# Float64 weights decoded with a parametric ReLU on ScalarE

## Chip, cores and metric

One Trainium2 chip, one of its cores. The metric is the device time of one execution of the program in microseconds; lower is better. PE is TensorE (matmuls; PEld its weight loads), DVE VectorE, ACT ScalarE, POOL GpSimd and SP the engine that issues the DMAs here. L92 is line 92 of the kernel file.

## What is computed

Three layers in a row, in float32 for the activations and with float64 weights:

```python
# attention inside chunks of 64 rows: q, k, v of 8 x 8 x 576 x 64
scores = q_c @ k_c.T / 8;  attn = softmax(scores);  x = attn @ v_c        # -> 8 x 576 x 512
# gated layer with a causal depthwise convolution of 5 taps
gate = sigmoid(sum(conv_w[k] * shift(x, k)));  x = (gate * (x @ w_val)) @ w_out   # 512 x 512 each
# feed-forward with layer norm, 512 -> 2048 -> 512
xn = (x - mean) / sqrt(var + 1e-6) * g_ln;  out = x + relu(xn @ w_ch1) @ w_ch2
```

w_val, conv_w, w_out, g_ln, w_ch1 and w_ch2 may come as float64. The chip gets the 64 bits of such a number as two 32-bit words, a low and a high one.

## The kernel before

**Precision.** Every operand of a large matmul is split in a high part, rounded to the type fp32r, and a low part, the rest. A product takes three matmuls: high by high, high by low, low by high.

**Decoding a weight.** A raw tile of 128 x 512 pairs of words comes by DMA (tag `raw`, two buffers in each pool). Four steps make a float32 tile `a` (tag `da`, three buffers) of it: ACT reads the high word as a float32, whose eight exponent bits are the upper eight of the float64's eleven, and multiplies it by 2^-112 (L87). That clears the top three exponent bits, so that DVE can shift the word left by three (L91). The shift throws the sign out. DVE takes the sign bit out of the high word and ORs it in (L92), then shifts the low word right by 29 and ORs that in (L93). `parts` then makes the two matmul operands: ACT rounds `a` to the high part (L100), POOL subtracts for the low part (L101). For the first feed-forward matrix, SP stores `a` to DRAM (L147) for later use.

**Where decodes run.** 41 times: once small (20 x 128) for the convolution's taps, four times for w_val and four times for w_out in the first 60 us, and 32 times for the feed-forward, two tiles `raw1` and `raw2` for each of 16 slices f of the hidden dimension. The first four slices are decoded when the last block's convolution is done (`early_ff`, issued after `last_tap`), the others by `next_ff` while the first block of rows runs through the feed-forward.

**Stages on PE.** Up to about 290 us: attention, convolution and gated layer, block by block (9 blocks of 512 rows), software-pipelined in `period`. From 290 to 313 us the last projection (`proj`) and the transposes of the first normalised rows. From 313 us the first block's feed-forward: per slice f, `ff1` (12 matmuls into `psh`, then hh on ACT L454 and hl on DVE L455) and `ff2` of an earlier slice (12 matmuls into `acc`), with the layer norm and the transposes of the next rows between them (`ln_rows`, `turn_rows`: the ACT scalings L425 and L435). From 417 us the other eight blocks, two at a time, in eight pairs of slices (`ff_pair`), where a Winograd-like scheme takes 7 products for 8: `make_pair` builds its weight combinations from the stored `a` on DVE (L521 to L524), ACT and POOL (L477, L478); `right_operands` builds those of the rows (L546, L478); inside a pair, `copy` (ACT L626), `add` (DVE L630) and `relu` (ACT L621, DVE L622) stand between the products.

**Order.** PE's order is written out by hand throughout, DVE's and ACT's too in the periods. Elsewhere a planner orders each engine's instructions ahead of time by its own costs and by priorities. Each engine, and SP's DMA queue, runs its instructions in order, so one that waits holds all those behind it.

Of the kernel before, what the change touches and what calls it, by code (L numbers as in the profile page):

```python
# [8 lines left out]
F32 = mybir.dt.float32  # L9
F32R = mybir.dt.float32r  # L10
U32 = mybir.dt.uint32
ACTF = mybir.ActivationFunctionType
ALU = mybir.AluOpType
# [6 lines left out]
def tile_chunk_attention_gated_mlp(ctx: ExitStack, tc: tile.TileContext, qk, v, w_val, conv_w, w_out, g_ln, w1, w2, out):  # L20
    nc = tc.nc
# [22 lines left out]
    scale = 1.0 / float(D) ** 0.5  # L44
# [39 lines left out]
        nc.sync.dma_start(out=t.rearrange("p c h d -> p (c h d)"), in_=v[u])  # L84

    def decode_copy(raw, a):
        nc.scalar.activation(out=a, in_=raw[:, :, 1].bitcast(F32), func=ACTF.Copy, scale=2.0 ** -112)  # L87

    def decode_bits(raw, a):
        lw, hw, au = raw[:, :, 0], raw[:, :, 1], a.bitcast(U32)  # L90
        nc.vector.tensor_scalar(out=au, in0=au, scalar1=3, scalar2=None, op0=ALU.logical_shift_left)  # L91
        nc.vector.scalar_tensor_tensor(out=au, in0=hw, scalar=0x80000000, in1=au, op0=ALU.bitwise_and, op1=ALU.bitwise_or)  # L92
        nc.vector.scalar_tensor_tensor(out=au, in0=lw, scalar=29, in1=au, op0=ALU.logical_shift_right, op1=ALU.bitwise_or)  # L93

    def decode(raw, a):
        decode_copy(raw, a)
        decode_bits(raw, a)
# [611 lines left out]
    def ff_copy(k):  # L709
        a = fa[k] = stg.tile([P, DM], F32, tag="da", name="da", bufs=3)  # L710
        decode_copy(wraw[k // 2][k % 2], a)

    def ff_bits(k):
        decode_bits(wraw[k // 2][k % 2], fa[k])
# [306 lines left out]
```

## Time and profile before

| | before |
|---|---|
| three runs, median (lowest to highest) | 1103.33 us (1102.24 to 1105.18) |
| profiled execution, time | 1105.21 us |
| its span, first to last instruction | 1103.4 us |
| mean granted PE clock | 0.989 |
| PE busy | 1058.8 us (96%), 6778 matmuls |
| DVE busy | 698.6 us (63%), 1107 instructions |
| ACT busy | 499.6 us (45%), 872 instructions |
| POOL busy | 106.2 us (10%), 120 instructions |

The profile is of one execution. Busy times are sums over the whole span; a granted clock of 1.00 is 2.4 GHz and 0.50 is 1.2 GHz.

### The profile page before, as it was taken

The numbers are of one execution on the slowest core, as the hardware profiler recorded it, in microseconds if no ns is written. First come the engines' busy times: TensorE is split into PE (matmuls) and PEld (weight loads), VectorE is DVE, ScalarE is ACT, GpSimd is POOL, SyncE is SP. The second block draws the span as 40 slices with busy tenths as digits, with TensorE's granted clock in tenths as the row PEclk, the third lists the DMA queues.
The fourth block names the chain that finished last, engine by engine and source line by source line (L and its number), as shares of the span: only waits on it lengthen the run. The fifth ranks groups of instructions, "written<-read, shape, count | busy, mean of one in ns | idle before, by whom it ended". The sixth has DMA issues, their size and how long they took to land.

```text
span 1103.4 us, 16877 instructions
## 1 busy us (share of the span) xinstructions
PE 1058.8 (96%) x6778; PEld 862.9 (78%) x6778; DVE 698.6 (63%) x1107; ACT 499.6 (45%) x872; POOL 106.2 (10%) x120
## 2 busy tenths in 40 slices
PE   4899999999899898999999999999999999999998
PEld 3578888888677676888888888888888888888887
DVE  5899999997969987556638335448334447433434
ACT  5777777776756654344433233433233323222221
POOL 1210000000124444222200000000000000000000
PEclk9999999999999898999999999999999999999999
DMA  9534344412387745333335523323533224522211
GB/s 374 204 140 144 136 144 154 144 59 78 115 280 234 240 162 219 134 116 134 135 136 167 173 96 115 117 93 125 200 103 108 97 85 132 194 94 96 77 39 76
DMA packets 58725, 156.32 MB, mean 142 GB/s; under 512 B 5758, under 2 KB 13974, under 8 KB 56214
## 3 DMA queue, kind: packets, MB, share of 16 engines
q1 hardware_dynamic: 58646, 155.23, 40.7%
q8 instruction: 53, 0.87, 0.3%
q14 instruction: 26, 0.21, 0.1%
HBM read 117.46 MB, written 37.75 MB: 141 GB/s over the span
## 4 chain that ended last, share of the span: by engine, by line
PE 79%; DVE 12%; ACT 3%; DMA 3%; issue 2%; POOL 1%; SPq 0%; ACTq 0%; DVEq 0%; POOLq 0%
PE x L610 16%; PE acc L584 16%; PE psf L584 15%; PE zy L610 9%; PE pso L335 8%; PE psv L335 8%; PE sc L175 2%; PE x L250 2%; DVE da L92 2%; DVE h L622 2%; PE pst L218 1%; DMA qkr<-in_qk 1%; DVE da L93 1%; PE pst L433 1%; DVE xt L546 1%
## 5 line engine op out<-in xcount | busy, mean ns | idle before, releaser
L630 DVE TENSOR_TENSOR c<-x,c 128x512 f32<-128x512 f32 x96 | 66.2, 690 | 235.5 <-ACT c L626 179.6
L584 PE MATMUL acc<-w,h 128*128 128x512 f32 x768 | 184.5, 390 | 0.0
L584 PE MATMUL psf<-w,h 128*128 128x512 f32 x768 | 184.3, 389 | 0.0
L584 PEld LDWEIGHTS acc<-w,h 128*128 128x128 f32 x768 | 144.3, 188 | 30.1
L584 PEld LDWEIGHTS psf<-w,h 128*128 128x128 f32 x768 | 144.3, 188 | 29.8
L610 PE MATMUL x<-t,wc 128*128 128x512 f32 x576 | 149.0, 395 | 4.6 <-DVE c L630 4.6
L626 ACT ACTIVATE c<-zy 128x512 f32<-128x512 f32 x96 | 57.8, 602 | 185.2 <-PE zy L610 185.1
L610 PEld LDWEIGHTS x<-t,wc 128*128 128x128 f32 x576 | 109.3, 190 | 28.8 <-DVE c L630 6.2
L621 ACT ACTIVATE h<-c 128x512 fp32r<-128x512 f32 x96 | 60.6, 631 | 134.8 <-DVE c L630 134.2
L589 DVE TENSOR_TENSOR yt<-psf,yt 128x512 f32<-128x512 f32 x128 | 88.1, 690 | 23.5 <-PE psf L584 20.7
L304 DVE SCALAR_TENSOR_TENSOR cg<-xf,cw,cg 128x516 f32<-128x516 f32 (+1 forms) x136 | 100.4, 752 | 3.0
L610 PE MATMUL zy<-b,wc 128*128 128x512 f32 x384 | 99.1, 394 | 0.0
L610 PEld LDWEIGHTS zy<-b,wc 128*128 128x128 f32 x384 | 71.7, 189 | 14.4
L622 DVE SCALAR_TENSOR_TENSOR h<-c,h 128x512 fp32r<-128x512 f32 x96 | 68.0, 708 | 11.2 <-ACT h L621 10.9
L335 PE MATMUL pso<-oh,gh 128*128 128x512 f32 x144 | 58.3, 405 | 1.8 <-ACT gh L371 1.8
L335 PE MATMUL psv<-xh,vh 128*128 128x512 f32 x144 | 59.2, 411 | 0.0
L335 PE MATMUL pso<-oh,gl 128*128 128x512 f32 x144 | 56.9, 395 | 1.9 <-DVE gl L374 1.9
L101 POOL TENSOR_TENSOR w<-da,w 128x512 fp32r<-128x512 f32 x32 | 46.1, 1447 | 114.7 <-ACT w L100 108.7
L335 PE MATMUL pso<-ol,gh 128*128 128x512 f32 x144 | 56.6, 393 | 0.0
L335 PE MATMUL psv<-xl,vh 128*128 128x512 f32 x144 | 56.6, 393 | 0.0
L335 PE MATMUL psv<-xh,vl 128*128 128x512 f32 x144 | 56.6, 393 | 0.0
L621 ACT ACTIVATE h<-x 128x512 fp32r<-128x512 f32 x32 | 19.2, 598 | 81.3 <-PE x L610 81.3
(114 smaller groups left out, 1591.9 us busy)
## 6 DMA issues: line engine op xcount, KB each, us to landing
wc<-wc SPq DMA_DIRECT2D x112, 512.0 KB, 3.2
qkr<-in_qk SPq DMA_DIRECT2D x19, 1024.0 KB, 7.4
raw<-in_moe_w_ch SPq DMA_DIRECT2D x32, 512.0 KB, 4.4
vr<-in_v SPq DMA_DIRECT2D x18, 512.0 KB, 4.2
yd<-y SPq DMA_DIRECT2D x36, 256.0 KB, 2.0
out<-yt SPq DMA_DIRECT2D x36, 256.0 KB, 3.7
yr<-yd SPq DMA_DIRECT2D x32, 256.0 KB, 3.2
yt<-yd SPq DMA_DIRECT2D x32, 256.0 KB, 3.7
```

Source lines behind the costliest of these rows:

```text
L92: nc.vector.scalar_tensor_tensor(out=au, in0=hw, scalar=0x80000000, in1=au, op0=ALU.bitwise_and, op1=ALU.bitwise_or)
L101: nc.gpsimd.tensor_tensor(out=lo, in0=a, in1=hi, op=ALU.subtract)
L175: nc.tensor.matmul(out=ps[CH * c:CH * c + CH, par, g, :], lhsT=qt[r0:r0 + CH, hp, cs], rhs=kt[r0:r0 + CH, hp, cs], start=True, stop=True,)
L304: last_tap[j] = nc.vector.scalar_tensor_tensor(out=o, in0=xf[j][:, f, i:i + n], scalar=cw[:, i * CT + f:i * CT + f + 1], in1=o, op0=ALU.mu ...
L335: nc.tensor.matmul(out=ps, lhsT=lt, rhs=rh, start=(i == 0), stop=(i == n - 1))
L584: nc.tensor.matmul(out=ps, lhsT=lt, rhs=rh, start=(g == 0 and k == 0 and (first or half)), stop=(g == 1 and k == 2 and (last or half)),)
L589: nc.vector.tensor_tensor(out=yt[i], in0=ps, in1=yt[i], op=ALU.add)
L610: nc.tensor.matmul(out=ps, lhsT=lt, rhs=rh, start=(start and c == 0 and i == 0), stop=(c == 1 and i == 2), skip_group_check=True)
L621: nc.scalar.activation(out=t[:, 0, :], in_=src, func=ACTF.Relu)
L622: nc.vector.scalar_tensor_tensor(out=t[:, 1, :], in0=src, scalar=0.0, in1=t[:, 0, :], op0=ALU.max, op1=ALU.subtract)
L626: nc.scalar.activation(out=t, in_=zy, func=ACTF.Copy)
L630: nc.vector.tensor_tensor(out=t, in0=x, in1=t, op=ALU.add)
```

## The change

The multiplication by 2^-112 on ACT becomes a parametric ReLU with the same scale and a slope of 2^32 for negative inputs. A negative number then comes out with 32 added to its exponent, which sets the exponent bit that the left shift by three moves into the place of the sign. So the shift gives the sign as well, and DVE's L92 is left out: a decode has three instructions on ACT and DVE before `parts` where it had four.

```diff
     def decode_copy(raw, a):
-        nc.scalar.activation(out=a, in_=raw[:, :, 1].bitcast(F32), func=ACTF.Copy, scale=2.0 ** -112)
+        nc.scalar.activation(out=a, in_=raw[:, :, 1].bitcast(F32), func=ACTF.Prelu, scale=2.0 ** -112, alpha=2.0 ** 32)
 
     def decode_bits(raw, a):
-        lw, hw, au = raw[:, :, 0], raw[:, :, 1], a.bitcast(U32)
+        lw, au = raw[:, :, 0], a.bitcast(U32)
         nc.vector.tensor_scalar(out=au, in0=au, scalar1=3, scalar2=None, op0=ALU.logical_shift_left)
-        nc.vector.scalar_tensor_tensor(out=au, in0=hw, scalar=0x80000000, in1=au, op0=ALU.bitwise_and, op1=ALU.bitwise_or)
         nc.vector.scalar_tensor_tensor(out=au, in0=lw, scalar=29, in1=au, op0=ALU.logical_shift_right, op1=ALU.bitwise_or)
```

## Rows read from the trace of the kernel before

**Rows 1.** The page's slices: busy tenths of PE and DVE in 40 slices.

```profile
...
PE   4899999999899898999999999999999999999998
...
DVE  5899999997969987556638335448334447433434
...
```

**Rows 2.** Stages: length; PE, PEld, DVE, ACT, POOL busy; clock; DMA; GB/s.

```profile
...
313.00:329.50 16.50, 16.50 (x73) 13.36 (x72) 11.51 (x24) 9.17 (x15) 5.31 (x4) 1.00 0.89 286
329.50:338.20 8.70, 5.32 (x20) 4.07 (x20) 7.90 (x18) 4.56 (x9) 2.59 (x2) 0.80 0.82 261
338.20:370.00 31.80, 31.80 (x151) 26.38 (x149) 31.63 (x61) 21.15 (x47) 14.64 (x10) 1.00 0.76 242
370.00:384.50 14.50, 9.45 (x33) 7.41 (x33) 13.19 (x17) 10.32 (x23) 7.53 (x5) 0.76 0.71 231
384.50:402.70 18.20, 16.96 (x75) 13.36 (x73) 15.90 (x25) 8.93 (x21) 7.47 (x6) 1.00 0.61 203
...
417.30:440.00 22.70, 17.61 (x62) 12.83 (x61) 15.87 (x25) 9.08 (x20) 9.74 (x12) 0.85 0.70 266
...
```

**Rows 3.** Groups by line, 313 to 403 us: busy, mean ns, idle before.

```profile
...
L101 POOL TENSOR_TENSOR w<-da,w 128x512 fp32r<-128x512 f32 x27 | 38.6, 1437 | 54.6 <-ACT w L100 48.6 <-issue 6.0
...
L92 DVE SCALAR_TENSOR_TENSOR da<-raw,da 128x512 uint32<-128x512 uint32 x26 | 24.7, 953 | 0.3
...
L87 ACT ACTIVATE da<-raw 128x512 f32<-128x512 f32 x26 | 17.2, 668 | 3.9 <-DMA raw<-in_moe_w_ch 3.9
...
```

**Rows 4.** Busy time by stage, instructions of L92 alone.

```profile
...
338.20:370.00 31.80, 10.02 (x11) 1.00 0.76 242
370.00:384.50 14.50, 6.60 (x6) 0.76 0.71 231
...
```

**Rows 5.** PE's waits, 284 to 440 us: total us, times, longest.

```profile
...
PE x L610 <- DVE c L630: 4.6, 3, 2.6
PE pst L433 <- ACT xt L435: 3.4, 1, 3.4
PE psh L335 <- ACT w L100: 2.8, 1, 2.8
PE pso L335 <- DVE gl L374: 1.9, 1, 1.9
...
PE psh L335 <- DVE hl L455: 1.7, 1, 1.7
...
```

**Rows 6.** Groups by line of the whole program, ACT.

```profile
...
L425 ACT ACTIVATE yr<-yr,w,r 128x512 f32<-128x512 f32 x32 | 24.4, 808 | 20.0 <-DVE w L423 19.9
...
L621 ACT ACTIVATE h<-x 128x512 fp32r<-128x512 f32 x32 | 19.2, 598 | 81.3 <-PE x L610 81.3
...
L198 ACT ACT_TABLE_LOAD x7 | 9.0, 1283 | 0.1
...
```

**Rows 7.** The line L92: ns shortest, median, longest.

```profile
...
L92 DVE SCALAR_TENSOR_TENSOR da<-raw,da x40: 650/692/1770, 11.4 to 399.9; 128x512 uint32<-128x512 uint32 x40
...
```

**Rows 8.** Timeline of DVE, 9 to 25 us: start, length.

```profile
...
10.47 0.28 DVE L92 SCALAR_TENSOR_TENSOR cwr<-cwu,cwr 20x128 uint32<-20x128 uint32 x1
...
11.44 0.69 DVE L92 SCALAR_TENSOR_TENSOR da<-raw,da 128x512 uint32<-128x512 uint32 x1
...
```

**Rows 9.** Chain that ended last, 9 to 24 us: start, length.

```profile
...
12.47 10.62 DMA qkr<-in_qk
...
23.13 1.23 PE x L284 x2
```

**Rows 10.** Chain that ended last, 57 to 63 us.

```profile
...
58.57 1.28 ACT L198
...
```

**Rows 11.** Timeline of DVE, 306 to 330 us.

```profile
...
324.92 0.69 DVE L92 SCALAR_TENSOR_TENSOR da<-raw,da 128x512 uint32<-128x512 uint32 x1
...
```

**Rows 12.** Timeline of ACT, 375 to 390 us.

```profile
...
376.21 0.63 ACT L100 ACTIVATE w<-da 128x512 fp32r<-128x512 f32 x1 [0.91 <-DVE da L93]
...
378.29 0.36 ACT L435 ACTIVATE xt<-pst,cw 128x128 f32<-128x128 f32 x1
...
```

## Prediction

> **What bounds the kernel.** I read the page's slices first. PE is busy in 39 of the 40 slices at eight tenths or more, and DVE is full in slices 3 to 9 and again in slices 13 to 15, from 331 to 414 us [rows 1]. A change that only relieves DVE can therefore gain nothing except where PE waits, so the next view is the busy time by stage around those slices, where the last weights (the feed-forward's) are decoded while the first block runs [rows 2]. The stretch from 313 to 329.5 us sets the pace: 73 matmuls in 16.5 us at clock 1.00 and without a gap, 0.226 us each. At that pace the 20 matmuls of the next stretch need 4.5 of its 8.7 us, so 4.2 us are lost there. The 33 of 370 to 384.5 need 7.5 of 14.5: 7.0 lost. The 75 of 384.5 to 402.7 need 17.0 of 18.2: 1.2 lost. These are the least that is lost, as some of the matmuls are short transposes. Between them, from 338.2 to 370, PE is never idle, but DVE has only 0.17 of 31.80 us free. From 417.3 to 440 another 8.7 us go (62 matmuls). Part of each loss is the clock: 0.80, 0.76 and 0.85 in the three bad stretches. The granted clock falls from 2.4 towards 1.2 GHz after PE has been kept waiting, so a wait that goes takes its slow matmuls with it.
>
> What the decode costs there is in the groups by line [rows 3]: from 313 to 403 us the merge of the sign, L92, takes 24.7 us of DVE in 26 instructions. The stretches of L92 alone say how much stands in the full queue: 11 before 370 and 6 up to 384.5 [rows 4]. The view of PE's waits names who ends them [rows 5]: the scaling of the transposed rows xt L435 (3.4 us), the high half of a weight w L100 (2.8), hl L455 (1.7), gl L374 (1.9), and c L630 (4.6 in three).
>
> **The change, part by part.** Removed: 41 L92 instructions (40 of 128x512, and the small one of the convolution's weights). Nothing is added to DVE. On ACT, 41 Copy become 41 Prelu at the same place. The trace has no Prelu. Below it stands Relu into h, 598 ns, above it the 128x512 ACTIVATE with two per-partition operands, 808 ns [rows 6]; the Copy it replaces takes 668 [rows 3]. I take 668, since scale and slope are both plain numbers; the dearer end would add 0.14 us to each of 26 in a stage where ACT is busy 54 of 90 us (the sum over 313 to 402.7 in [rows 2]), so it hides. No DMA, tile or buffer moves, but both successors do: L93 can start one instruction earlier, and with it w L100, POOL's w L101, the store of a and, as L93 is the last reader of raw, the next weight load on SP's queue.
>
> How long is one removed L92? Its mean in the stage is 953 ns, yet its shortest is 650 and its median over the program 692, its longest 1770 [rows 3, 7]; the long ones run beside POOL's L101, of 1437 ns each. If that wait belongs to L92, 24.7 us go; if L93, which stands behind it and also reads two SBUF tensors, inherits it, only 26 x 0.69 = 18.0 go. I count 0.69, which goes in either case; with the whole record term 5 below would reach its upper bound, 7.0, and the sum 13.0 in place of 11.5. Both figures are above the 12.4 us (4.2 + 7.0 + 1.2) that PE loses in the stage, so the cap on the gain is what PE loses and not the DVE time that comes free. The Trainium skill, SBUF — State Buffer, section "SBUF: two separate sides", says that VectorE and GpSimd hold a shared port pair for a whole instruction, so the loser waits it out. By that rule the wait passes on to L93, which speaks for 18.0 and the sum of 11.5, and makes the change worth less than the row's mean says; the spread from 650 to 1770 ns agrees with such waits, and who inherits them only the changed kernel can show.
>
> The terms, in order of time:
> (1) Start. DVE runs an L92 of 0.28 and one of 0.69 us [rows 8] ahead of the first normalisation, for which PE's first transposes wait. PE then runs into the next load of q and k, which lands at 12.47 + 10.62 = 23.09 [rows 9]; PE starts the matmuls just ahead of those that need it at 23.13 and takes 1.2 us for them, so about 1 us of earlier work still counts. 1.0; bounds 0 and 1.0.
> (2) Around 60 us PE waits for a chain of POOL ol, ACT, a table load and the exponential [rows 10]. No L92 is in it, so nothing; at most 2 x 0.69 = 1.4 for the two L92 ahead of that chain's inputs.
> (3) Last projection, 299 to 303 us: gl L374 stands on DVE behind an L92 and the split of xn. 0.6; bounds 0 and the whole wait, 1.9.
> (4) 329.5 to 338.2: the awaited weight has its decode on DVE among those of its neighbours. Three L92 like the one shown stand ahead of it from 322 to 330 us [rows 11], 2.1 us, and with the stall shortened part of the slow matmuls goes. 2.5 of 4.2; at least 0.7 (the weight's own L92).
> (5) 370 to 384.5: ACT sits 0.91 us for L93 before L100 at 376.21 and reaches xt L435 only at 378.29 [rows 12], where PE waits. What is late is the whole DVE queue: 17 L92, 17 x 0.69 = 11.7 us, stand in it from 338.2 on, more than the 7.0 lost. Not all of it reaches PE, because raw loads and ACT's own order hold some. 5.5; bounds 1.4 (the two nearest) and 7.0.
> (6) 384.5 to 402.7: 0.9 of 1.2; bounds 0 and 1.2.
> (7) 417.3 to 440: the first pair has no other matmuls to cover its ACT and DVE round trip, so most stays. The late first L630 stands behind the preparation that began when the decode ended. 1.0 of 8.7; at most the 4.6 of the waits on L630, and as a loss 2, if PE gets there first and waits longer.
> Elsewhere (90 to 290 us, and after 440) PE covers everything [rows 1]: removed DVE work there is worth nothing. It is worth nothing in term 4 to 6 either once PE's waits are gone.
> Sum: 1.0 + 0 + 0.6 + 2.5 + 5.5 + 0.9 + 1.0 = 11.5. The profiled execution took 1105.2 us, 1.8 more than its span of 1103.4; it becomes 1093.7. The median of the runs is 1103.3, 1.9 below, so the forecast for it is 1091.8, say 1092. All lower bounds: 0 + 0 + 0 + 0.7 + 1.4 + 0 - 2 = 0.1, so 1103. All upper: 1.0 + 1.4 + 1.9 + 4.2 + 7.0 + 1.2 + 4.6 = 21.3, so 1082.
>
> **Rivals.** (a) The waits stay because the weights arrive late, not because DVE is slow: raw buffers and SP's order set the pace. For it: ACT's decode does wait for raw at times, and DMA engines are 61 to 89% busy in the stage [rows 2]. Against: the highest share, 0.89, stands in the stretch without any loss, and PE loses most at 0.71; raw is also freed by L93. Then only 1.0 + 0.6 + 0.7 + 1.4 = 3.7 come: 1099.6.
> (b) Everything named goes, as DVE, with 18 us less, no longer holds ACT anywhere, and the preparation of the pairs starts earlier too. For it: 11.7 freed against 7.0 lost. Against: in (4) and (7) ACT, POOL and loads are in the chain as well. About 20: 1083.
> (c) Slower: Prelu is not in the table that is loaded, and each decode brings loads. One load is 1.283 us on ACT [rows 6]. Two for each of 26 decodes would be 52 x 1.283 = 66.7; ACT has 89.7 - 54.1 = 35.6 idle in the stage, so from 28 loads on it is the bound, and at 52 it is 31 over: 1134. The program has 19 loads: seven stand ahead of Exp, as shown, and the others ahead of Sigmoid, Sqrt and the very first activation; Relu and Copy alternate through the main part without one, so I hold Prelu for a function of their kind. The Trainium skill, ScalarE: Activation LUTs, section "Table sets: the hidden batching unit", says that cheap functions are in every set (it names relu, copy, identity and abs, not Prelu), and that a switch costs about 2.7 us; by its rule for a function outside the set the 26 switches there and back would be an estimated 140 us of ACT. No row here settles it. A milder way to the same side is left in this chance: ACT, DVE and POOL are ordered by a planner that will plan anew.
> That the change does nothing at all is excluded in count: 41 instructions leave DVE.
>
> **How the numbers follow.** Forecast (gains of 7 to 16) 0.62; (a) 0.20; (b) 0.12; (c) with its milder way 0.06. A measurement of this kernel tells 0.3%, 3.3 us, from no change: 1100.0 and 1106.6 are the edges. Faster: 0.62 + 0.12 + half of (a), whose 1099.6 lies on the edge, about 0.84; same: the other half, 0.10; slower 0.06. Range: from the sum of upper bounds, 1082, to 1101, which takes in (a)'s time and most of its spread.
>
> **What would show it.** Right: DVE has 41 instructions fewer and 28 to 35 us less busy; L87 stays near 0.67 us with no load ahead of it; the stretch that now runs from 313 to 403 is 8 to 11 us shorter, its clock near 1.00 and the waits on w L100 and xt L435 under 1 us each. Term 5 is wrong if xt L435 still holds PE while DVE has idle time; then (a), with waits of ACT on raw. (b) shows as c L630 off the list of waits. (c) shows as more than 19 table loads. The prediction fails most easily by a new order in which some other DVE instruction, waiting for POOL, stands in front of what PE needs.

## The result, and the profile after

The changed kernel takes 1092.37 us (median of 4 runs, 1091.54 to 1093.75), the kernel before 1102.89 beside it (4 runs, 1102.24 to 1105.18): a ratio of 0.990, 95% interval 0.988 to 0.992. The forecast was 1092. Behind L92 every line number is one lower than before: the low word's OR is now L92, the ReLU still L87, the shift L91, the high part L99, POOL's low part L100, hh L453, hl L454, xt L434, c L629.

The profiled execution took 1091.69 us, 13.5 less than the one of before. That one lay at the top of its runs, so it shows 3 us more than the medians' 10.5. DVE is busy 669.7 us in 1066 instructions, 28.9 us and 41 instructions less.

First the stages, cut where PE starts the same matmul as at the borders of [rows 2], give or take two; the fifth row ends where 402.7 stood. Columns as there.

```profile
309.10:325.50 16.40, 16.40 (x74) 13.59 (x73) 8.88 (x18) 8.70 (x15) 3.89 (x3) 1.00 0.83 277
325.50:330.84 5.34, 3.87 (x22) 2.82 (x20) 5.15 (x11) 3.48 (x6) 2.54 (x2) 1.00 0.89 294
330.84:363.00 32.16, 32.11 (x152) 26.53 (x151) 26.18 (x59) 25.59 (x56) 16.01 (x12) 1.00 0.81 262
363.00:370.79 7.79, 6.56 (x34) 5.08 (x32) 6.34 (x10) 6.46 (x17) 4.54 (x4) 1.00 0.85 275
370.79:392.37 21.58, 17.08 (x74) 13.46 (x74) 14.72 (x21) 12.27 (x26) 9.42 (x9) 1.00 0.62 207
...
405.97:426.60 20.63, 17.20 (x61) 12.86 (x60) 13.82 (x23) 8.74 (x20) 9.79 (x12) 0.83 0.71 272
```

The two bad stretches of before have shrunk, from 8.70 to 5.34 and from 14.50 to 7.79 us, and their clock went from 0.80 and 0.76 to 1.00 [rows 2]. In the third stretch PE was full and still is, but DVE now has 6 of 32 us free, where it had 0.17. The fifth stretch is new trouble: 18.20 us long before, 21.58 now, with 74 matmuls that need 16.7 at 0.226 each. From 313 to 402.7 us it was 89.70 us in all, and now it is 83.27:

```profile
313.00:402.70 89.70, 80.04 (x346) 64.57 (x345) 80.13 (x142) 54.14 (x112) 37.55 (x27) 0.94 0.75 242
309.10:392.37 83.27, 76.02 (x346) 61.49 (x345) 61.28 (x117) 56.51 (x116) 36.40 (x28) 1.00 0.77 254
```

PE's waits from 279 to 428 us (the stretch of [rows 5]) name it:

```profile
PE x L609 <- DVE c L629: 3.4, 2, 2.6
PE psh L334 <- DVE hl L454: 3.3, 1, 3.3
PE pso L334 <- DVE gl L373: 1.8, 2, 1.6
PE pst L432 <- ACT yr L424: 1.4, 1, 1.4
...
PE pst L432 <- ACT xt L434: 1.2, 1, 1.2
PE acc L469 <- DVE hl L454: 1.2, 1, 1.2
```

The wait on a weight's high half (2.8 us before) is off the list, and xt went from 3.4 to 1.2. In their place stand one of 3.3 and one of 1.2 us on hl L454, both in the fifth stretch. The chain that ended last in the window from 370 to 381 us (start, length) shows how the first comes about:

```profile
...
373.10 0.63 ACT w L99
373.73 0.56 ACT da L87
374.30 0.02 issue
374.32 1.08 DVE da L91
375.40 0.02 issue
375.42 0.70 DVE da L92
376.13 0.02 issue
376.15 0.02 ACT w L99
...
```

Neither engine is the bound here: ACT and DVE wait for one another. ACT rounds a tile (L99), decodes the next (L87), DVE does the bits (L91, L92), and ACT waits for them with the next L99: 3.05 us a tile, from 373.10 to 376.15. hh L453, which hl and so PE need, comes behind such a pair on ACT, at 377.24, and ends at 377.82. Then hl waits once more, on DVE (timelines of DVE and POOL):

```profile
377.36 1.10 DVE L91 TENSOR_SCALAR da<-da 128x512 uint32<-128x512 uint32 x1 [1.25 <-ACT da L87]
378.49 0.69 DVE L92 SCALAR_TENSOR_TENSOR da<-raw,da 128x512 uint32<-128x512 uint32 x1
379.10 0.68 DVE L454 SCALAR_TENSOR_TENSOR hl<-psh,hh 128x512 fp32r<-128x512 f32 x1
...
384.04 1.42 DVE L520 TENSOR_TENSOR raws<-raws 128x256 f32<-128x256 f32 x1 [0.62 <-DMA raws<-ad]
...
386.51 0.68 DVE L454 SCALAR_TENSOR_TENSOR hl<-psh,hh 128x512 fp32r<-128x512 f32 x1
```

```profile
376.91 1.27 POOL L100 TENSOR_TENSOR w<-da,w 128x512 fp32r<-128x512 f32 x1 [1.80 <-issue]
...
383.89 1.29 POOL L100 TENSOR_TENSOR w<-da,w 128x512 fp32r<-128x512 f32 x1 [2.67 <-issue]
```

A shift L91 of 1.10 us and an L92 stand ahead of hl, and ahead of the next hl an L520 of 1.42 us, of the preparation of the pairs. Both long ones run beside POOL's L100. The 27 large L91 of this trace that run without one take 0.41 to 0.43 us, the 13 beside one 0.42 to 1.52; an L520 takes 0.42 at its shortest.

The groups of DVE in the whole stage, 309.1 to 392.37 us (busy, mean ns, idle before), say the same of ACT and DVE, and below them the row of L91 before:

```profile
L92 DVE SCALAR_TENSOR_TENSOR da<-raw,da 128x512 uint32<-128x512 uint32 x26 | 21.2, 820 | 0.5
L91 DVE TENSOR_SCALAR da<-da 128x512 uint32<-128x512 uint32 x26 | 15.8, 614 | 15.3 <-ACT da L87 15.2
```

```profile
L91 DVE TENSOR_SCALAR da<-da 128x512 uint32<-128x512 uint32 x26 | 13.6, 525 | 3.6 <-ACT da L87 3.6
```

DVE sits 15.3 us idle ahead of L91, against 3.6 before.

On ACT the ReLU costs what the copy did, and the table loads are 8, 7, 2, 1 and 1, as many as before, 19 (groups of ACT, whole program, the three smallest of the loads left out):

```profile
L87 ACT ACTIVATE da<-raw 128x512 f32<-128x512 f32 x40 | 26.0, 665 | 9.2 <-DMA raw<-in_moe_w_ch 7.1 <-DMA raw<-in_moe_w_val 1.3 <-POOL ol L100 0.6
L309 ACT ACT_TABLE_LOAD x8 | 10.3, 1283 | 0.1
L197 ACT ACT_TABLE_LOAD x7 | 9.0, 1283 | 0.1
...
```

One more difference is in no diff: the planner has ordered ACT, DVE, POOL and SP anew. Laid beside each other without L92 and the table loads, the two traces have another instruction at 107 of DVE's 1066 places, at 111 of ACT's 853, at 48 of SP's 361 transfers and at 2 of POOL's 120 (buffer numbers left out). PE's order is the same. The larger counts in the first expectation below do not agree with the traces.

### The profile page after: what moved, and what is told of

Its sections match the earlier page's. It is cut to its first block, busy times and chain, and to the rows that moved or that the text cites. A ratio compares the mean times of both kernels' runs of the same rounds, so it can differ in the third digit from the quotient of the medians.

```text
span 1089.9 us, 16844 instructions
## 1 busy us (share of the span) xinstructions
PE 1051.0 (96%) x6778; PEld 857.0 (79%) x6778; DVE 669.7 (61%) x1066; ACT 499.5 (46%) x872; POOL 102.8 (9%) x120
## 4 chain that ended last, share of the span: by engine, by line
PE 80%; DVE 10%; ACT 4%; DMA 4%; issue 1%; SPq 0%; ACTq 0%; DVEq 0%
PE x L609 16%; PE acc L583 16%; PE psf L583 15%; PE zy L609 10%; PE pso L334 8%; PE psv L334 8%; PE sc L174 2%; DMA raw<-in_moe_w_ch 2%; DVE h L621 2%; PE x L249 2%; DMA qkr<-in_qk 1%; DVE cg L303 1%; PE pst L217 1%; PE acc L469 1%; DVE da L92 1%
## 5 line engine op out<-in xcount | busy, mean ns | idle before, releaser
L629 DVE TENSOR_TENSOR c<-x,c 128x512 f32<-128x512 f32 x96 | 66.3, 690 | 236.0 <-ACT c L625 180.2
L588 DVE TENSOR_TENSOR yt<-psf,yt 128x512 f32<-128x512 f32 x128 | 88.2, 691 | 23.5 <-PE psf L583 20.7
L477 POOL TENSOR_TENSOR wc<-raws,wc 128x256 fp32r<-128x256 f32 x56 | 45.6, 836 | 101.6 <-ACT wc L476 96.6
```

The costliest lines, as they stand in the source:

```text
L477: eng.tensor_tensor(out=lo, in0=a, in1=hi, op=ALU.subtract)
L588: nc.vector.tensor_tensor(out=yt[i], in0=ps, in1=yt[i], op=ALU.add)
L629: nc.vector.tensor_tensor(out=t, in0=x, in1=t, op=ALU.add)
```

## The experiments

Twelve kernels ran, each timed beside the kernel before on the same chip. That kernel's median was 1104.15 us for the first four runs, 1104.69 for the next four, 1104.28 for the next three, and 1103.54 for the last one. The groups ran on different chips, so a difference of a microsecond or two between kernels of different groups is not settled. Theory: the gain is DVE's time, freed where the feed-forward's weights are decoded. Rivals: it comes from the new order, from the shorter chain of a tile, or from the early weights.

### Order and instruction, apart

Two kernels separate them. The program is built twice, and the order that the first build gets on DVE, ACT, POOL and SP is laid on the second by order-only dependencies (shortened):

```diff
+    _, order = program(ORDER_OF_MERGE)       # True: with L92, as before
+    nc, got = program(MERGE, order)          # False: with the ReLU, without L92
...
+                    for a, b in zip(line, line[1:]):
+                        tc.add_manual_dep(b, a.name, NoSync, reason="order")
```

> The changed kernel's instructions, but every engine and SP's queue held to the order that the planner gave the kernel before (L92 simply missing from DVE's). Theory A, the prediction's: the time comes from DVE's freed time in the order as it was. Then the full gain is here, 1091 to 1094 us. Theory B: the gain comes from the planner's new order (after the change 960 of some 950 rows on DVE and 589 of 640 on ACT differ in a line-by-line comparison; the exponential's table load near 60 us moved from behind the weights' chain to 4.9 us earlier). Then most of it is missing, 1098 to 1103 us.

Measured: 1088.65 us (1085.16 to 1090.00), ratio 0.986 [0.984, 0.988]. The old order keeps the whole gain and adds 3.7 us to it by the medians (5.0 when each is set against the kernel before beside it). So the gain is not the planner's, and this is the fastest kernel of the study, together with one below. In its profiled execution the stage from the first psh to the end of the decodes, 89.70 us before, looks like this (windows):

```profile
305.85:383.85 78.00, 75.17 (x346) 61.71 (x345) 59.42 (x116) 55.33 (x114) 37.63 (x28) 1.00 0.85 278
```

It is 11.7 us shorter: of the 12.4 that PE lost there before, nearly all came back. This execution, 1085.16 us, is the fastest of its four, but two others in the same order on DVE, f1 and g2 below, lie 12.9 and 12.1 us shorter between the same matmuls. (12.4 is not a hard cap: it was the least that PE lost.) ACT's idle time has changed hands (groups of ACT in it, then the rounding before):

```profile
L91 ACT ACTIVATE da<-raw 128x512 f32<-128x512 f32 x26 | 17.4, 668 | 9.7 <-DMA raw<-in_moe_w_ch 8.9 <-POOL w L107 0.7
L106 ACT ACTIVATE w<-da 128x512 fp32r<-128x512 f32 x26 | 16.2, 628 | 7.4 <-DVE da L99 7.2
```

```profile
L100 ACT ACTIVATE w<-da 128x512 fp32r<-128x512 f32 x26 | 16.3, 630 | 20.5 <-DVE da L93 20.4
```

Here L106, the rounding, waits 7.2 us for DVE (20.4 before, 17.4 in the changed kernel), and the ReLU 8.9 for raw loads (3.9 before). The loads may be the next limit; no run tests that.

The mirror image keeps the merge and takes the changed kernel's order:

> The opposite: the kernel before with L92, Copy on ACT, but every engine in the order of the changed kernel, each L92 directly ahead of its L93. Theory A: DVE has as much to do as before, so 1100 to 1104 us. Theory B: the order alone brings most, 1092 to 1096 us.

Measured: 1117.41 us (1116.97 to 1118.45), ratio 1.012 [1.011, 1.014]. The order that the planner made for a program without L92 is 13 us worse when L92 is there. Its longest waits of PE between 284 and 440 us are 8.7 us in five on xt and 5.7 in two on hl.

### Which weights

Late weights alone (the 32 of the feed-forward), then early ones alone (the nine up to 60 us), each ordered by the planner:

```diff
+        if late[0] == PRELU_LATE:
             ... func=ACTF.Prelu, scale=2.0 ** -112, alpha=2.0 ** 32
+        else:
             ... func=ACTF.Copy, scale=2.0 ** -112
...
+        if late[0] != PRELU_LATE:
             ...                                       # L92
```

> Only the 32 decodes of the feed-forward weights are changed; the 9 early ones keep Copy and L92. The prediction's terms 3 to 7 (10.5 of 11.5) give 1102.9 - 10.5 = 1092.4 us. The two traces, laid beside each other by PE's landmarks, put 4.6 us of the gain ahead of 290 us, where only the 9 early decodes were changed: by that 1097 us.

> Only the 9 early decodes are changed, the 32 of the feed-forward keep Copy and L92. The prediction's terms 1 and 2 give 1102.9 - 1.0 = 1101.9 us; the landmarks of the two traces give 1102.9 - 4.6 = 1098.3 us.

Measured: 1093.48 us (1092.15 to 1094.91), ratio 0.991 [0.989, 0.992]; and 1102.05 (1100.97 to 1105.01), ratio 0.998 [0.997, 0.999]. The feed-forward's decodes carry 10.7 us, the early ones 2.1. Both times are those of the prediction's terms (1092.4 and 1101.9), not those of the landmarks (1097 and 1098.3).

The same split with the order of before held:

```diff
-ORDER_OF_MERGE, MERGE = True, False
+ORDER_OF_MERGE, MERGE = (True, True), (True, False)   # L92 kept in (early, late)
```

> The kernel before's order on DVE, ACT, POOL and SP is kept (as in o1_after_in_before_order, 1088.65 us), and only the 32 feed-forward decodes lose the merge L92; the nine early ones keep it. Beside f2 it tells what each half is worth when no new order is mixed in. By the landmarks on PE in the profiled execution of o1, 5.9 us of its gain lie before the feed-forward begins, so theory A (the two halves add) expects 1088.65 + 5.9 = 1094.5 us, with 1092.5 to 1096.5 taken for agreement. The rival (what the early decodes give shows at the start but is lost later, as the 2.1 us of e3_prelu_in_first_weights suggest) expects 1090.7, within 1089.5 to 1092.

> The mirror of f1: the kernel before's order is kept, the nine early decodes lose L92 and the 32 feed-forward ones keep it. Theory A (the halves add) expects 1104.15 - 5.9 = 1098.3 us. The rival expects 1102, as in e3_prelu_in_first_weights. If the early half is worth nothing at all, 1104.

Measured: 1091.22 us (1090.02 to 1091.73), ratio 0.988 [0.987, 0.990], where the feed-forward's decodes lose L92; and 1104.62 (1101.53 to 1106.66), ratio 1.000 [0.999, 1.001], where the early ones do. So 13.5 us come from the former and nothing from the latter alone. My theory that the two halves add fell by 3.3 and 6.3 us. The profile of the second shows why not to read a gain off an early landmark: PE is 3.8 us ahead when the feed-forward begins, 2.0 ahead at the end of the decodes, 0.7 ahead in the last stages. The stage takes 91.39 us there (89.70 before), with DVE still busy for 80.4 us of it (80.1 before); what holds PE back in it, step by step, I did not settle. Another 1.6 us go behind it: PE waits 2.3 us for h L631 on DVE up to 437.64, which it did not before, and the clock of the next 20 us is 0.91 (1.00 in the same place before). With both halves the early one is worth 1091.22 - 1088.65 = 2.6; that is a difference between two chips, and the two ratios' intervals touch, so it may be nothing.

### DVE's time or the length of the chain

```diff
         nc.vector.scalar_tensor_tensor(out=au, in0=lw, scalar=29, in1=au, ...)
+        nc.vector.scalar_tensor_tensor(out=hw, in0=hw, scalar=0x80000000, in1=hw,
+                                       op0=ALU.bitwise_and, op1=ALU.bitwise_or)
```

> The kernel before's order and the parametric ReLU, but each decode gets an instruction of L92's form back on DVE, behind L93, that writes the raw tile's own high words and that nothing of the decode waits for. So DVE is as busy as before, while the chain ACT, DVE, ACT of a tile is one instruction shorter. Theory A (what counts is DVE's time, since DVE is full where the weights are decoded) expects the whole gain to be lost: 1102 to 1107 us. Rival (what counts is the length of a tile's chain, in which ACT and DVE wait for one another) expects it to stay: 1088 to 1092. A value between tells the shares.

Measured: 1100.91 us (1099.45 to 1103.94), ratio 0.998 [0.997, 0.999]. Of the 16.0 us between the kernel before (1104.69) and the one in its order without L92 (1088.65), 12.3 are gone again, though nothing of the decode waits for the added instruction. DVE's groups from 310.85 to 398.30 us:

```profile
L101 DVE SCALAR_TENSOR_TENSOR raw<-raw 128x512 uint32<-128x512 uint32 x26 | 21.0, 807 | 0.0
L99 DVE SCALAR_TENSOR_TENSOR da<-raw,da 128x512 uint32<-128x512 uint32 x26 | 20.7, 795 | 0.1
L95 DVE TENSOR_SCALAR da<-da 128x512 uint32<-128x512 uint32 x26 | 18.6, 717 | 2.9 <-ACT da L91 2.8
```

The three together are 60.3 us, as L91, L92 and L93 were before (13.6 + 24.7 + 21.8 = 60.1): the dummy restores DVE's load, and three quarters of the time come back with it. The other 3.8 us by the medians (0.9 to 3.8 by the ratio's interval) are the share of the shorter chain. One rival this leaves: the dummy also holds the raw tile, and SP's next load into it waits for the dummy (10.1 us in four waits in this trace), as it waited for L93 before. So the 12.3 us are DVE's time and the earlier release of the raw tile together. That DVE's time is the larger of the two is argued, not shown: before, ACT stood 20.4 us for DVE's bits ahead of the rounding and 3.9 us for raw loads ahead of the decode.

### The instruction on ACT by itself

```diff
-        ... func=ACTF.Copy, scale=2.0 ** -112)
+        ... func=ACTF.Prelu, scale=2.0 ** -112, alpha=1.0)     # L92 stays
```

> The kernel before with the parametric ReLU at a slope of 1 in place of the copy, and the merge L92 kept: the instruction on ACT alone, with the same order on every engine. Theory A (on ACT the one costs what the other does, and no table is loaded for it) expects no change: 1101 to 1107 us, L87 at 0.66 to 0.68 us, 19 table loads. Rival c of the prediction (the parametric ReLU brings table loads of some 1.28 us) expects 1134, and a milder form (L87 longer by 0.1 to 0.2 us) 1107 to 1111.

Measured: 1103.67 us (1101.80 to 1104.96), ratio 0.999 [0.998, 1.000]. L87 takes 671 ns (670 before), and there are 19 table loads. Rival (c) in its main form is out. Its profiled execution is 2.3 us shorter than that of the kernel before, with the same order and nothing taken off DVE: so much can lie between two single executions.

### What the new order costs

> The changed kernel with ACT alone held to the order of the kernel before; the planner orders DVE and SP anew around it (POOL comes out in the order of the kernel before by itself). Which engine's new order costs the 3.7 us between the changed kernel (1092.37) and o1_after_in_before_order (1088.65)? Theory A (ACT's: PE waits 3.3 us for hl because hh stands behind a weight's rounding and the next weight's ReLU in ACT's new order) expects 1087 to 1090. Rival (DVE's, or the order of the loads on SP) expects 1091.5 to 1094.

> The changed kernel with DVE alone held to the order of the kernel before; ACT, POOL and SP are ordered anew. Theory A (ACT's order) expects 1091.5 to 1094, the rival (DVE's order) 1087 to 1090. Both at 1088 would say that each one's order repairs the other's.

> The changed kernel with SP alone, which issues the loads and stores, held to the order of the kernel before; DVE, ACT and POOL are ordered anew. Theory A (ACT's order) expects 1091.5 to 1094, the rival (the order of the loads) 1087 to 1090.

Each is the kernel of the first experiment with fewer engines held (shortened):

```diff
-    ENG = {DVE, Activation, Pool, SP}
+    ENG = {Activation}          # g1;  {DVE} in g2;  {SP} in g3
```

Measured: 1099.20 us (1097.76 to 1101.28), ratio 0.995 [0.994, 0.997], with ACT's order held; 1088.65 (1088.45 to 1093.56), 0.986 [0.984, 0.988], with DVE's; 1094.08 (1092.01 to 1095.92), 0.991 [0.989, 0.992], with SP's. My theory (ACT's order) fell, by 10 us: to hold DVE's order of before is enough for the 3.7 us, and to hold ACT's alone is worse than either whole order. The planner's answers differ, though: around DVE's order of before it puts SP's back in all but 13 of 361 places and gives ACT a third order (56 places off the one of before, 83 off the changed kernel's); around ACT's it gives DVE a third one (100 and 94). So the runs show which engine to hold, not that the others' orders count for nothing. The traces fit: the two hl of the fifth stretch, which start 1.29 and 2.27 us after their hh in the changed kernel, start 0.91 and 0.78 after it with DVE held. PE's longest wait and a piece of the chain that ended last, with ACT held:

```profile
PE psh L341 <- ACT w L106: 6.9, 1, 6.9
...
```

```profile
318.49 5.93 DMA raw<-in_moe_w_ch
...
331.28 0.16 DVE w L429
331.51 0.68 issue
332.19 0.80 ACT yr L431
332.98 0.53 ACT w L106
```

A raw load lands at 324.4, 5.9 us after the step before it in the chain. Then the rounding that PE needs, the L106 at 332.98, stands on ACT behind two scalings L431 that wait for the layer norm's small instructions on DVE (L429). Here one engine's order held against another's newly planned one has made such a wait.

A last kernel decodes the two tiles of a slice side by side in the program and leaves the order to the planner:

```diff
...
+        decode_copy(r1, a)
+        decode_copy(r2, b)
+        decode_bits(r1, a)
+        decode_bits(r2, b)
+        parts(t[:, 0, :], t[:, 1, :], a)
...
+        parts(t[:, 0, :], t[:, 1, :], b)
```

> The changed kernel with the two tiles of a feed-forward slice decoded side by side in the program: both ReLUs, both bit steps, then both roundings, where the changed kernel writes one tile's four steps and then the other's. The planner orders every engine anew. In the changed kernel's trace at 373 to 379 us one tile goes at a time, ACT and DVE waiting for one another, 3.0 us a tile. Theory A (that costs the 3.7 us to o1_after_in_before_order, and two tiles side by side cure it) expects 1087 to 1090. Rival (the planner draws another order with losses of its own elsewhere, so what the program writes decides little) expects 1091 to 1096.

Measured: 1091.86 us (1091.48 to 1093.08), ratio 0.989 [0.988, 0.991], the changed kernel's own time within its runs. The rival holds: the planner's order has 3.6 us of waits on hl again. Between the matmuls of the fifth stretch this trace is 1.8 us shorter than the changed kernel's, and from 309.1 us to there it is 2.0 longer, so side by side helps where it was meant to and costs as much elsewhere. That the to and fro between ACT and DVE from 373 to 379 us is what the new order costs is therefore seen in one trace, not shown.

## Why the prediction was right

The time, the count of 41, the engine and the place were right: 1093.48 with the feed-forward's decodes alone, 1100.91 with a dummy behind L93, 1103.67 with the ReLU alone. The terms, read from where PE starts the same matmul in both profiled executions, add up to 13.5 where 11.5 was forecast (10.5 by the medians). That the sum came so near is in part luck: 3.6 us too little for the start and 4.4 too much for term 6 cancel. Of the prediction's own signs, DVE's (28.9 us less), the ReLU's, the clock's and the wait on w hold; the stage is 6.4 us shorter and not 8 to 11, and xt still holds PE for 1.2 us and not under 1.

Single executions differ, so no term is good to better than one or two us: the kernel with the ReLU alone, same order and L92 kept, reads 1.1 us ahead of the one before at 283 us, 0.2 behind at 313 and 1.6 ahead at 402.7. The three traces with DVE in the order of before that have no L92 in the stage (o1, f1, g2) agree better with one another: 1.3 for term 3, 2.7 to 3.5 for term 4, 7.2 to 7.7 for term 5, 1.6 to 1.7 for term 6 and 0.1 for term 7. There terms 3 to 6 come above their forecasts, 5 and 6 above their bounds too, as the losses that set these were least values; and term 7 does not come.

- Terms 1 and 2 (1.0 and 0): 4.6 us up to 283 us, above the sum of their upper bounds, 2.4. Term 1's landmark was right: the load of q and k lands at 12.47 + 10.90 = 23.37 in the chain below, and PE is 0.8 ahead at the next matmuls, at 23.51. The step that failed is "no L92 is in it, so nothing" for the stretch up to 60 us: PE's lead grows by tenths at the hand-overs and inside runs of matmuls, to 3.1 at the product of the transposed attention weights at 59.28 (62.40 before), and then to 4.6, as the stretch from 57 to 66 us runs at clock 1.00 (0.87 before). The bound looked only at the chain that ended last, and that one has changed: from 45 to 59 us it runs mostly over DVE, without POOL's ol and without the table load of [rows 10]. The lead is no fixed thing: with the same nine decodes relieved it is 5.9 us at this landmark in o1 and -0.2 in g2. At the end of the program it is worth 0 to 2.6 us (f2, e3, o1 less f1), so the forecast of 1.0 was nearer to the time than to the landmark.

  The chain that ended last, after, 19 to 66 us:

```profile
12.47 10.90 DMA qkr<-in_qk
...
55.57 1.14 DVE ex L190
56.74 1.06 ACT ex L197
57.80 0.52 ACT gh L370
58.32 0.92 ACT pT L223
...
59.28 1.16 PE x L249 x64
```

- Term 3 (0.6): -0.7, less than single executions differ by. gl L373 still holds PE for 1.8 us in the waits above (1.9 in [rows 5]), so the step failed in the new order. In the old one it holds: the stretch gains 1.3, and gl's wait is 1.3 there.
- Term 4 (2.5): 3.4, with the clock from 0.80 to 1.00, as argued. The wait on w is gone; a new one of 1.4 us on yr stands there.
- Term 5 (5.5): 6.5 of the 7.0, net of 0.3 that the stretch ahead of it lost.
- Term 6 (0.9): -3.5, the new waits of 3.3 and 1.2 us on hl. This is the failure that the prediction named last: DVE instructions that take longer beside POOL's L100 (the L91 of 1.10 and the L520 of 1.42 us above) stand in front of the hl that PE needs. It was named and had no term in the sum. With the order of before the same stretch gains 1.7 us.
- Term 7 (1.0): 2.0; c L629 still holds PE for 3.4 us (4.6 in [rows 5]), the first of its three waits having gone. In the order of before all three are there (4.6 us in o1), though the decodes end earlier still. So the step that takes this wait for a debt of the late decode failed, and the 2.0 came with the new order. Another 1.0, between the old 402.7 and 417.3 us, stands in no term.
- L92's price: I counted 0.69, with 0.95 as the record. Seven of the 40 records explain the mean: they take 1.65 to 1.77 us, each beside a POOL L101. In the order of before, with the same other instructions, DVE's busy time in the stage falls from 80.13 to 59.42, or 20.7 / 26 = 0.80 each (0.77 in f1, 0.87 in g2). Of the 6.7 us that the records held beyond 0.69, 2.7 went and 4.0 moved, in o1 most of it to the shift (13.6 to 16.0 us) and not, as the prediction has it, to L93 (21.8 to 22.2); in f1 both grow. The Trainium skill, SBUF — State Buffer, section "SBUF: two separate sides", has VectorE and GpSimd shut each other out of a shared port pair for a whole instruction; the trace agrees that such waits move to the neighbours, but not all of them do. In the changed kernel itself, where one more large DVE instruction falls into the stage, the fall is 18.9.
- Rival (a), loads: off at 1099.6, though ACT's waits for raw grew. Rival (b): 1083 was not reached, though the lowest run in the order of before, 1085.16, came near; there the stage does give back nearly all, as (b) has it, and c L636 still holds PE for 4.6 us. Rival (c): out by its table loads. In its milder form, the order, it is real: that order costs 13 us with L92 and 3.7 without it, less than the gain.
- A reading of [rows 1]: DVE's slice 11 stands at nine tenths too, and its slice 15 at eight and not full. No term uses either.

## What to carry to other kernels

Where an engine is full in one stage and PE waits there, count the removed time of that stage, cap it by what PE loses, and expect little from the same edit elsewhere: a lead at an early landmark can be lost again in the next full stage. Where a planner orders the engines, an edit of one instruction is also a new order: time the edit in the old order too, which here was worth another 3.7 us, and choose the engines to hold by measurement: DVE alone did as well as all four, and ACT alone was 10 us behind them.

## What was not expected of the hardware

A parametric ReLU of 128x512 on ACT takes 671 ns where a copy with a scale takes 670, and it brings no table load. The record of a DVE instruction can hold waits that do not all go with it: 0.80 of the recorded 0.95 us went. With PE's losses down from 4.2 and 7.0 us to under 0.5 each by the same 0.226 us a matmul, the two bad stretches show a clock of 1.00, where they had 0.80 and 0.76.
